# Attention numerators stored head-within-row, product banks tied to set slots of an instruction string, and the output products of the second weights in banks of four and two pieces

## The chip, the cores and the metric

The kernel runs on one core of a Trainium2 chip. The metric is the device time of one launch in microseconds (us). Five engines run their own instruction queues in order: PE (matmul), DVE (vector), ACT (activation), POOL (GpSimd) and SP, which here only issues DMAs. They meet only through semaphores.

## The reference

```python
def mha(x, wqkv, wo):                  # B=1, S=2048, D=512, H=32, Dh=16, float32
    q, k, v = split_heads(x @ wqkv)
    p = softmax(einsum("bhqd,bhkd->bhqk", q, k) * Dh ** -0.5)
    return merge_heads(einsum("bhqk,bhkd->bhqd", p, v)) @ wo

g = sigmoid((x * gate_w).sum(-1, keepdims=True))
out = g * mha(x, wqkv_a, wo_a) + (1 - g) * mha(x, wqkv_b, wo_b)
```

## The kernel before

**The work.** There are 64 heads (32 of each block), in 8 groups G of 8. For a head, two things are done for each tile of 128 tokens, called a round (1024 rounds in all). First the maximum of each query's scores is found: six plain maxima and one paired maximum for two rounds (`max_plain`, L229; `max_rise` and `max_pair`, L236 and L241). ACT and DVE share this. Later the scores are computed again with keys on partitions, shifted by the maxima, and put through Exp on ACT (`score`, L292 and L294). The result is multiplied with V and a column of ones on PE (`attend`, L875), in one PSUM bank `acc`. Rows 0 to 15 of each of four strips of `acc` are numerators, row 16 is the softmax denominator. Each half of a head's queries ends with a copy `ev<-acc` (L898) and a store to a DRAM tensor `od` (L899).

**The maxima's way back.** `max_split` (L252 on DVE, L253 to L255 on POOL) splits half a head's maxima into two fp16 parts. `max_rows` transposes them on DVE (L259), writes them to DRAM (`md<-mt`, L262) and reads them back as two further rows of `q_st` (L265). The scores of that half head wait for them.

**The string.** One pass of the string `FULL` covers four rounds and fixes the order of all engines' work: `e` is one score bank with its Exp (16 in a pass), `m`, `D` and `A` are steps of the maxima, a digit is so many quarters of an `attend`, and `W` (four in a pass) is a slot for one piece of the hidden products. `E` evicts a finished product bank. `W` and `R` also run one entry of `row_ops`, which holds `max_split` and `max_rows`. Every second `e` issues one DMA of the list `waiting`, which I call a drip. The last 14 rounds use the string `LATE`.

**The hidden products.** The generator `hidden` puts the projections of later groups, and then the output products, into the slots `W`. A bank is 8 pieces (L311, L333, L618), collected in the single PSUM buffer `ps_p`; `bank` makes sure that the bank before is evicted before the next begins. Evictions alternate between ACT (L735) and DVE (L736) through `copier`. The output products come in five parts: groups 0 to 3 for each half of the tokens (16 banks of 8 pieces, evicted by `first`), then the second weights' groups 4 and 5 for the upper half (8 banks of 4), 4 to 6 for the lower half (8 banks of 6), and 6 for the upper half (8 banks of 2), all evicted by `more` on DVE (L815). Group 7 is handled in the tail by code of its own (`LAST`).

**What feeds the output products.** `prepared` loads the numerators of a group and half of the tokens (`load_num`: four DMAs into `ot`, four into `o_part`) and the inverse denominators (`load_rb`: four DMAs `rb<-rd`), adds the two key halves on POOL (`add_num`, L608) and multiplies (`normalize`, L612). These DMAs go through the same drip and the same SP queue as `md<-mt` and `q_st<-md`. The access patterns before:

```python
od[g]: [HG, 2, NQ, 32, 512]                                                     # L75
load_num: ap=[[2 * NQ * 32 * 512, 4], [512, DH], [1, 512]]                      # L593
load_rb:  ap=[[S, 4], [0, DH], [1, 512]]                                        # L603
```

Of the kernel before, what the change touches and what calls it, by code (L numbers as in the profile page):

```python
# [23 lines left out]
F32 = mybir.dt.float32  # L24
# [9 lines left out]
P = 128  # L34
# [20 lines left out]
def gated_mha(ctx: ExitStack, tc: tile.TileContext, xT, x, wqkv_a, wo_a, wqkv_b, wo_b, gate_w, out):  # L55
# [76 lines left out]
    def drip_rows(t, src, n, last=KH):  # L132
        waiting.extend((part_rows, t, src, b, k, n) for k in range(0, last, n) for b in HALVES)

    def mark(name):
        flags[name] = now[0]

    flags, now = {}, [0]

# [393 lines left out]
    def load_den(G):  # L533
        o, n = od[G], gh[G] * DH
        for part in range(2):
            dens[G, part] = work.tile([P, P], F32, name=f"dn{part}")
            for c in range(2):
                nc.sync.dma_start(dens[G, part][c * 64:c * 64 + n // 2],
                                  bass.AP(tensor=o.tensor, offset=o.offset + (32 * (2 * part + c) + 16) * 512,
                                          ap=[[NQ * 32 * 512, gh[G] * 2], [P, 4], [1, P]]))  # L540
# [38 lines left out]
    def load_num(G, i):  # L579
        k = SLOTS[G, i]  # L580
        o = od[G]
        for p in range(2):
            for f, b in enumerate((64, 0)):
                for hh in range(2):
                    def one(p=p, f=f, b=b, hh=hh):
                        if (p, f, hh) == (0, 0, 0):
                            nums["p", G, i] = T["late"].tile([P, 2, 512], F32, name="o_part", bufs=2)
                            nums["r", G, i] = T["late"].tile([P, 2, 512], F32, name="rb", bufs=2)
                        nc.sync.dma_start(
                            nums["p", G, i][b:b + 64, hh] if p else T["o"][b:b + 64, k + hh],  # L590
                            bass.AP(tensor=o.tensor,
                                    offset=o.offset + ((4 * hh * 2 + i) * 4 + 2 * p + f) * 32 * 512,
                                    ap=[[2 * NQ * 32 * 512, 4], [512, DH], [1, 512]]))  # L593
                    yield one

    def load_rb(G, i):
        r = rd[G]
        for f, b in enumerate((64, 0)):
            for hh in range(2):
                def one(f=f, b=b, hh=hh):  # L600
                    nc.sync.dma_start(nums["r", G, i][b:b + 64, hh],
                                      bass.AP(tensor=r.tensor, offset=r.offset + 4 * hh * S + i * 1024 + f * 512,
                                              ap=[[S, 4], [0, DH], [1, 512]]))  # L603
                yield one
# [117 lines left out]

    def bank(pieces, evict):
        empty()
        ps = ps_p.tile([P, 512], F32, name="ps_p")
# [17 lines left out]
    def prepared():  # L743
        added = []
        for name, jobs in (("phase", ((0, 0), (1, 0), (2, 0), (3, 0), (0, 1), (1, 1))),
# [3 lines left out]
            for G, i in jobs:  # L749
                yield from until((G + 1) * HG * NT + 26)  # L750
                while len(added) > 1 and now[0] < added[-2] + 3:
                    yield
                waiting.extend((fn,) for fn in (*load_num(G, i), *load_rb(G, i)))
                waiting.append((mark, ("in", G, i)))
                yield from wait(("in", G, i))
                r = now[0] + 6
                at(r, add_num, G, i)
                at(r + 2, normalize, G, i)
                added.append(r)
                flags["ready", G, i] = r + 5  # L760

    def hidden():
# [34 lines left out]
        drip_rows(w_big, wo[0], 1)  # L797
        for G in range(NG, 2 * NG):
# [14 lines left out]
        def more(ps, t):  # L813
            o = T["acc"][:, t]
            dve.scalar_tensor_tensor(o, ps, gate[1][:, t:t + 1], o, op0=ALU.mult, op1=ALU.add)  # L815

# [5 lines left out]
        flags["out", 0, 1] = now[0]  # L822
        drip_rows(w_big, wo[1], 1, 6)
        waiting.append((nc.sync.dma_start, w_big[:DH, 6], wo[1][DM - DH:, :]))
# [55 lines left out]
    def attended(u):  # L880
# [14 lines left out]
        elif h < NH - 1 and w % NT == NT - 1:  # L895
            G, j = divmod(h, HG)
            ev = work.tile([P, 512], F32, name="ev")
            (dve.tensor_copy if w < NT or h == NH - 2 else act.copy)(ev, acc)  # L898
            nc.sync.dma_start(od[G][j, w // NT].rearrange("c r t -> (c r) t"), ev)  # L899

# [15 lines left out]

    FULL = "mDmeE3We1e2me2A1em3em2em2eWE1D2me1m2em2emeW2e1mE1eme4WREReA"
    LATE = "e2We2e2EWe2e2e2EWe2e2E"
# [10 lines left out]
    while r < ROUNDS:  # L929
# [6 lines left out]
        if r % NT == 2 and r // NT + 1 < NH:  # L936
            new_maxima(r // NT + 1)
        scored = bursts = 0
        for code in order:
# [16 lines left out]
            elif code == "W":  # L956
                next(stream, None)
            elif code.isdigit():
                for _ in range(attend_next(int(code))):
# [46 lines left out]
```

## Time and profile before

| | us |
|---|---|
| runs | 2624.59, 2629.59 and 8974.59 |
| median | 2629.59 |
| the profiled execution | 2624.47 |
| its span, first to last instruction | 2622.6 |
| busy in it: PE, DVE, ACT, POOL | 2529.7, 2369.7, 2397.6, 411.5 |

The first launch took 8974.59 us; the median is not touched by it. A busy PE is not PE at its peak, since the ends of matmuls are modelled. ACT and DVE are busy 91% and 90% of the span, so the time is lost in stretches where both wait at once, and the question for each stretch is who waits for whom.

### The profile page before, as it was taken

To read this page: it belongs to the slowest core of one execution; us is meant where nothing else is said; L and a number is where in the kernel's file an instruction comes from. 1 tells how busy PE (TensorE), PEld (TensorE's weight loads), DVE (VectorE), ACT (ScalarE), POOL (GpSimd) and SP (SyncE) were. 2 spreads that over 40 slices of the span, in tenths; PEclk is the share of its full clock that TensorE was granted. 3 is DMA by queue.
4 is the path that set the end of the run, shared out by engine and by line. 5 is a ranking of instruction groups with operands and counts; after the bars stand their busy time and mean duration, and the time that the engine had idled before them with its cause. 6 is when DMAs were issued, how large, how long until landed. Compare 5 with 4: busy or idle time off the path is not lost.

```text
span 2622.6 us, 169689 instructions
## 1 busy us (share of the span) xinstructions
PE 2529.7 (96%) x76566; PEld 1608.1 (61%) x76566; DVE 2369.7 (90%) x4604; ACT 2397.6 (91%) x4741; POOL 411.5 (16%) x809
## 2 busy tenths in 40 slices
PE   8999999999999999999999999989999999899997
PEld 4566766666666666666666666545665665555663
DVE  2889999999999999999999999988899899899994
ACT  1589999999999999999999999989999999899995
POOL 2132211212100000211112111112101100101003
PEclk9899999999999999999999999999999999999999
DMA  7432323222221222323222222223113212212103
GB/s 156 110 85 74 86 65 93 82 71 58 71 60 52 74 65 62 88 73 79 61 66 74 69 62 65 80 89 108 47 50 97 84 50 77 80 54 83 34 27 115
DMA packets 144943, 195.09 MB, mean 74 GB/s; under 512 B 39752, under 2 KB 89880, under 8 KB 144216
## 3 DMA queue, kind: packets, MB, share of 16 engines
q1 hardware_dynamic: 138680, 172.82, 23.1%
q8 instruction: 599, 9.81, 1.6%
q0 software_dynamic: 2560, 8.91, 1.3%
q10 hardware_dynamic: 2976, 2.49, 0.4%
q14 instruction: 128, 1.05, 0.1%
HBM read 117.56 MB, written 66.58 MB: 70 GB/s over the span
## 4 chain that ended last, share of the span: by engine, by line
PE 75%; DVE 11%; DMA 4%; POOL 3%; ACT 3%; issue 2%; SPq 1%; ACTq 0%; POOLq 0%; DVEq 0%
PE acc L875 35%; PE ps_m L223 14%; PE ps_st L292 12%; DVE mxp L229 7%; PE ps_p L311 6%; PE ps_st L223 3%; PE ps_p L618 2%; DMA md<-mt 2%; ACT p L294 2%; PE ps_p L333 1%; DVE ev L898 1%; DVE rise L241 1%; ACT ev L898 1%; POOL stage L771 1%; DMA w<-in_wqkv_a 1%
## 5 line engine op out<-in xcount | busy, mean ns | idle before, releaser
L294 ACT ACTIVATE p<-ps_st 128x512 f32<-128x512 f32 x4068 | 2122.5, 640 | 105.3 <-PE ps_st L292 67.9
L875 PE MATMUL acc<-p,vg 64*17 64x384 f32 (+1 forms) x34784 | 2194.0, 366 | 12.2 <-DVE ev L891 2.4
L229 DVE TENSOR_REDUCE mxp<-ps_m 128x1 f32<-128x512 f32 x3072 | 1942.1, 683 | 89.7 <-PE ps_m L223 61.7
L292 PE MATMUL ps_st<-q_st,k_st 50*32 50x512 f16 x16272 | 1559.2, 382 | 24.1 <-DMA q_st<-md 21.7
L223 PE MATMUL ps_m<-k_st,q_st 48*32 48x512 f16 x14336 | 1384.1, 379 | 24.5 <-DVE mxp L229 20.5
L875 PEld LDWEIGHTS acc<-p,vg 64*17 64x17 f32 x34784 | 975.5, 93 | 236.8 <-DVE ev L898 23.1
L292 PEld LDWEIGHTS <-k_st 50*32 50x32 f16 x16384 | 664.5, 90 | 387.9 <-issue 191.7
L223 PEld LDWEIGHTS <-q_st 48*32 48x32 f16 x16384 | 553.4, 90 | 266.1 <-issue 172.6
L311 PE MATMUL ps_p<-x_sb,w 64*32 64x512 f32 x3648 | 478.2, 591 | 1.3 <-issue 0.8
L241 DVE CUSTOM_DVE_ANT_0 rise<-ps_m,rise 128x512 f32<-128x512 f32 x512 | 349.6, 683 | 64.3 <-PE ps_st L292 56.5
L236 ACT ACTIVATE rise<-ps_st 128x512 f32<-128x512 f32 x512 | 316.3, 618 | 41.7 <-PE ps_st L223 29.5
L618 PE MATMUL ps_p<-w_big,ot 64*32 64x512 f32 x1792 | 234.8, 591 | 14.1 <-DVE o_acc L815 12.2
L223 PE MATMUL ps_st<-x_st,q_st 48*32 48x512 f16 x2048 | 225.5, 379 | 1.1 <-DMA x_st<-xd 1.1
L253 POOL TENSOR_SCALAR mrow<-mrow 128x8 f32<-128x8 f32 x128 | 29.8, 233 | 1233.5 <-DVE mrow L252 1233.1
L357 POOL CAST parts<-stage 128x512 f16<-128x512 f32 x56 | 34.1, 610 | 853.8 <-DVE stage L736 434.2
L311 PE MATMUL ps_p<-w_big,x_sb 64*32 64x512 f32 x1024 | 134.2, 590 | 0.0
L311 PEld LDWEIGHTS ps_p<-x_sb,w 64*32 64x32 f32 x3648 | 116.7, 106 | 17.0 <-DMA w<-in_wqkv_a 1.8
L333 PE MATMUL ps_p<-w_big,x_sb 64*32 64x256 f32 x1280 | 88.6, 382 | 0.1
L618 PEld LDWEIGHTS ps_p<-w_big,ot 64*32 64x32 f32 x1792 | 54.3, 106 | 38.3 <-DVE o_acc L815 17.1
L358 POOL TENSOR_TENSOR parts<-stage,parts 128x512 f16<-128x512 f32 x56 | 65.3, 1165 | 4.5
L333 PEld LDWEIGHTS ps_p<-w_big,x_sb 64*32 64x32 f32 x1280 | 44.1, 107 | 12.8 <-issue 1.0
L898 DVE COPY ev<-acc 128x512 f32<-128x512 f32 x64 | 44.2, 691 | 1.2 <-PE acc L875 0.7
(107 smaller groups left out, 769.2 us busy)
## 6 DMA issues: line engine op xcount, KB each, us to landing
od<-ev SPq DMA_DIRECT2D x126, 256.0 KB
k_st<-kd SPq DMA_DIRECT2D x128, 128.0 KB
q_st<-qd SPq DMA_DIRECT2D x126, 128.0 KB
vd<-v_st SPq DMA_DIRECT2D x64, 136.0 KB
vg<-vd POOLq DMA_DIRECT2D x32, 272.0 KB, 4.1
k_st<-kd SPq DMA_DIRECT2D x128, 64.0 KB
q_st<-qd SPq DMA_DIRECT2D x126, 64.0 KB
kd<-parts SPq DMA_DIRECT2D x56, 128.0 KB
```

What stands on the lines that cost most here:

```text
L223: pe.matmul(ps[j:j + 32], q[b:b + SC, t * P + j:t * P + j + 32], k[b:b + SC], start=True, stop=True, tile_position=(b, j))
L229: dve.tensor_reduce(o[:, c:c + 1], ps, op=ALU.max, axis=AX.X)
L236: act.activation(rises[m], ps, AF.Relu)
L241: dve.tensor_tensor_reduce(out=rise, in0=ps, in1=rise, scale=1.0, scalar=LOWEST, op0=ALU.add, op1=ALU.max, accum_out=o[:, 0:1])
L292: pe.matmul(ps[j:j + 32], k[b:b + SC + 2, kk * P + j:kk * P + j + 32], qv(b), start=True, stop=True, tile_position=(b, j))
L294: act.activation(pt[u][:, c * 512:(c + 1) * 512], ps, AF.Exp, scale=SCALE / UNIT ** 2)
L311: pe.matmul(ps[j:j + 32], a, m, start=k == 0, stop=k == last, tile_position=(b, j))
L333: pe.matmul(ps[j:j + 32, e * 256:(e + 1) * 256], x_sb[b:b + 64, i, k, o:o + 32], w_big[b:b + 64, k, g * P:(g + 2) * P], start=k == e == 0, ...
L358: pool.tensor_tensor(t[:n, 1], v[:n], t[:n, 0], op=ALU.subtract)
L618: pe.matmul(ps[j:j + 32], T["o"][b:b + 64, k, o + j % 64:o + j % 64 + 32], w_big[b:b + 64, g], start=first, stop=last, tile_position=(b, j))
L875: pe.matmul(acc[d:d + 17, qa * P:qb * P], v[b:b + 64, 2 * (w % n) + c if h == NH - 1 else w % n, j], pt[u][b:b + 64, c * 512 + qa * P:c * ...
L898: (dve.tensor_copy if w < NT or h == NH - 2 else act.copy)(ev, acc)
```

## The change

Five edits.

1. `od` of groups 0 to 6 is stored as [half of the queries, half of the heads, strip, row, head, 512]. A partition of `ot` then holds row d and head j as 4d + j instead of 16j + d, and `wo` is loaded in the same order (`wo_rows`). `load_num` needs four DMAs of 256 KB for eight of 128 KB. The first dimension of the DRAM side becomes 64 for the numerators (4 before) and 16 for `rb` (4 before); for the denominators `dn` it becomes 4 (16 before).
2. `max_rows` runs one entry of `row_ops` later: an empty entry stands between `max_split` and `max_rows`.
3. Until the `LATE` string, a bank starts only at the first slot `W` of a pass, or at the third if it has two pieces.
4. The second weights' products become banks of 4 (groups 4 and 5, both halves) and of 2 (group 6, both halves): 32 banks for 24, with the same 96 pieces. `more` alternates between DVE as before and ACT with an addition on POOL.
5. `add_num` and `normalize` are issued together at set rounds, and one `E` of `FULL` moves by a few letters.

```diff
-    od = [dram.tile([HG, 2, NQ, 32, 512], F32, name=f"od{g}") for g in range(2 * NG)]
+    od = [dram.tile([2, 2, NQ, 32, HG // 2, 512], F32, name=f"od{g}") for g in range(2 * NG - 1)]
...
+    def wo_rows(src, b, k):
+        s = src[k * 64:(k + 1) * 64]
+        nc.sync.dma_start(w_big[b:b + 64, k], bass.AP(tensor=s.tensor, offset=s.offset,
+                                                      ap=[[DM, DH], [DH * DM, HG // 2], [1, DM]]))
...
+                    nc.sync.dma_start(dens[G, part][c * 64:(c + 1) * 64], bass.AP(
+                        tensor=o.tensor, offset=o.offset + ((2 * part + c) * 32 + DH) * (HG // 2) * 512,
+                        ap=[[step, 4], [P, DH], [1, P]]))
...
-                            nums["p", G, i][b:b + 64, hh] if p else T["o"][b:b + 64, k + hh],
-                            bass.AP(tensor=o.tensor,
-                                    offset=o.offset + ((4 * hh * 2 + i) * 4 + 2 * p + f) * 32 * 512,
-                                    ap=[[2 * NQ * 32 * 512, 4], [512, DH], [1, 512]]))
+                        nums["p", G, i][b:b + 64] if p else T["o"][b:b + 64, k:k + 2],
+                        bass.AP(tensor=o.tensor,
+                                offset=o.offset + 2 * i * step + (2 * p + f) * 32 * (HG // 2) * 512,
+                                ap=[[512, 64], [step, 2], [1, 512]]))
...
-                                              ap=[[S, 4], [0, DH], [1, 512]]))
+                                              ap=[[0, DH], [1024, HG // 2], [1, 512]]))
...
     def bank(pieces, evict):
+        while not ring and slot[0] % 4 != (2 if len(pieces) == 2 else 0):
+            yield
...
-                while len(added) > 1 and now[0] < added[-2] + 3:
+                while len(added) > 1 and now[0] < added[-2] + 4:
...
-                r = now[0] + 6
+                r = now[0] + 4
+                while r % 8 not in (4, 6) or added and r <= added[-1]:
+                    r += 1
                 at(r, add_num, G, i)
-                at(r + 2, normalize, G, i)
+                at(r, normalize, G, i)
...
         def more(ps, t):
...
+            turn[0] ^= 1
+            if turn[0]:
+                v = T["late"].tile([P, 512], F32, name="added", bufs=2)
+                act.activation(v, ps, AF.Copy, scale=g)
+                pool.tensor_tensor(o, o, v, op=ALU.add)
+            else:
+                dve.scalar_tensor_tensor(o, ps, g, o, op0=ALU.mult, op1=ALU.add)
...
-        yield from wait(("ready", 4, 1), ("ready", 5, 1))
-        yield from outs((4, 5), 1, more)
-        yield from wait(*(("ready", G, 0) for G in (4, 5, 6)))
-        yield from outs((4, 5, 6), 0, more)
-        yield from wait(("ready", 6, 1))
-        yield from outs((6,), 1, more)
+        for i in (1, 0):
+            yield from wait(("ready", 4, i), ("ready", 5, i))
+            yield from outs((4, 5), i, more)
+        for i in (0, 1):
+            yield from wait(("ready", 6, i))
+            yield from outs((6,), i, more)
...
-    FULL = "mDmeE3We1e2me2A1em3em2em2eWE1D2me1m2em2emeW2e1mE1eme4WREReA"
+    FULL = "mDmeE3We1e2me2A1em3em2em2eW1D2mEe1m2em2emeW2e1mE1eme4WREReA"
...
-            row_ops[0:0] = [(max_split, h, f // 8), (max_rows, h, f // 8)]
+            row_ops[0:0] = [(max_split, h, f // 8), (None,), (max_rows, h, f // 8)]
```

In the order of the built programs the change shows at three places on which the prediction rests. (In the changed kernel's rows lines are numbered anew: L252 is L261, L259 is L268, L229 is L238, L898 is L927, L735 is L756.)

The first place is DVE in the steady part, at the second half of head 26 (rows from `max_split`'s reduction `mrow` to the transpose `mt`); before:

```order
L252 TENSOR_REDUCE mrow<-mxp 128x8
L229 TENSOR_REDUCE mxp<-ps_m 128x1
L241 ISA rise,mxp<-ps_m,rise 128x512
L241 ISA mxp 128x1
L229 TENSOR_REDUCE mxp<-ps_m 128x1 x3
L259 STREAM_TRANSPOSE mt<-mparts_225 128x32
```

and with the change:

```order
L261 TENSOR_REDUCE mrow<-mxp 128x8
L238 TENSOR_REDUCE mxp<-ps_m 128x1
L250 ISA rise,mxp<-ps_m,rise 128x512
L250 ISA mxp 128x1
L238 TENSOR_REDUCE mxp<-ps_m 128x1 x7
L268 STREAM_TRANSPOSE mt<-mparts_225 128x32
```

The transpose moves back behind four more maxima.

The second place is SP, at the second half of head 42, where the kernel loads numerators (`ot`, `o_part`), inverse denominators (`rb`) and the next stacks (`k_st`, `q_st<-qd`) around the way back of the maxima; before:

```order
L601 DMA rb<-rd_117 64x1x512 x2
L589 DMA ot<-od_107 64x1x512 x4
L589 DMA o_part<-od_107 64x1x512 x4
L899 DMA od_110<-ev 128x512
L601 DMA rb<-rd_118 64x1x512 x4
L262 DMA md_113<-mt 4x32x32
L265 DMA q_st_211<-md_113 2x1024 x2
L106 DMA k_st_220<-kd_92 32x1x2048
L106 DMA q_st_219<-qd_84 32x1x2048
```

and with the change:

```order
L619 DMA rb<-rd_118 64x1x512 x2
L607 DMA ot<-od_108 64x2x512 x2
L607 DMA o_part<-od_108 64x2x512 x2
L932 DMA od_110<-ev 128x512
L619 DMA rb<-rd_119 64x1x512 x4
L107 DMA k_st_220<-kd_92 32x1x2048
L107 DMA q_st_219<-qd_84 32x1x2048
L271 DMA md_113<-mt 4x32x32
L274 DMA q_st_211<-md_113 2x1024 x2
```

The numerators take half as many DMAs of twice the size, and two loads of the next stacks now stand ahead of `md<-mt`.

The third place is ACT, at the third eviction that it does in the first weights' output products (`o_acc`), with the head's copy `ev`; before:

```order
L898 COPY ev<-acc 128x512
L294 ACTIVATE p<-ps_st 128x512
L236 ACTIVATE rise<-ps_st 128x512
L294 ACTIVATE p<-ps_st 128x512 x8
L236 ACTIVATE rise<-ps_st 128x512
L294 ACTIVATE p<-ps_st 128x512 x5
L735 ACTIVATE o_acc<-ps_p,gate_1578 128x512
L294 ACTIVATE p<-ps_st 128x512 x3
```

and with the change:

```order
L303 ACTIVATE p<-ps_st 128x512 x8
L245 ACTIVATE rise<-ps_st 128x512
L303 ACTIVATE p<-ps_st 128x512 x7
L927 COPY ev<-acc 128x512
L756 ACTIVATE o_acc<-ps_p,gate_1578 128x512
L303 ACTIVATE p<-ps_st 128x512
```

The eviction moves from the middle of a pass to its end, right behind the copy `ev`, which is on ACT in the same passes. On DVE its evictions fall behind DVE's copies `ev` in the same way.

More of the change, by code (lines that the diff above doesn't have):

```diff
@@ L133, in drip_rows, with drip_wo @@
         waiting.extend((part_rows, t, src, b, k, n) for k in range(0, last, n) for b in HALVES)
+    def wo_rows(src, b, k):
+        s = src[k * 64:(k + 1) * 64]
+        nc.sync.dma_start(w_big[b:b + 64, k], bass.AP(tensor=s.tensor, offset=s.offset,
+                                                      ap=[[DM, DH], [DH * DM, HG // 2], [1, DM]]))
+    def drip_wo(src, last=KH):
+        waiting.extend((wo_rows, src, b, k) for k in range(last) for b in HALVES)
     def mark(name):
         flags[name] = now[0]
-    flags, now = {}, [0]
+    flags, now, slot = {}, [0], [0]
     for k in range(0, KH, 2):
@@ L581, in load_num, with one @@
         o = od[G]
+        step = NQ * 32 * (HG // 2) * 512
         for p in range(2):
             for f, b in enumerate((64, 0)):
[L584 to L589, printed above, removed]
-                            nums["p", G, i][b:b + 64, hh] if p else T["o"][b:b + 64, k + hh],
-                            bass.AP(tensor=o.tensor,
-                                    offset=o.offset + ((4 * hh * 2 + i) * 4 + 2 * p + f) * 32 * 512,
-                                    ap=[[2 * NQ * 32 * 512, 4], [512, DH], [1, 512]]))
-                    yield one
+                def one(p=p, f=f, b=b):
+                    if (p, f) == (0, 0):
+                        nums["p", G, i] = T["late"].tile([P, 2, 512], F32, name="o_part", bufs=2)
+                        nums["r", G, i] = T["late"].tile([P, 2, 512], F32, name="rb", bufs=2)
+                    nc.sync.dma_start(
+                        nums["p", G, i][b:b + 64] if p else T["o"][b:b + 64, k:k + 2],
+                        bass.AP(tensor=o.tensor,
+                                offset=o.offset + 2 * i * step + (2 * p + f) * 32 * (HG // 2) * 512,
+                                ap=[[512, 64], [step, 2], [1, 512]]))
+                yield one
     def load_rb(G, i):
@@ L813, in more @@
         def more(ps, t):
-            o = T["acc"][:, t]
-            dve.scalar_tensor_tensor(o, ps, gate[1][:, t:t + 1], o, op0=ALU.mult, op1=ALU.add)
+            o, g = T["acc"][:, t], gate[1][:, t:t + 1]
+            turn[0] ^= 1
[5 more added lines that the diff above has]
+                dve.scalar_tensor_tensor(o, ps, g, o, op0=ALU.mult, op1=ALU.add)
         yield from wait(*(("ready", G, 0) for G in range(4)))
@@ L898, in attended @@
             (dve.tensor_copy if w < NT or h == NH - 2 else act.copy)(ev, acc)
-            nc.sync.dma_start(od[G][j, w // NT].rearrange("c r t -> (c r) t"), ev)
+            o = od[G]
+            if G == LAST:
+                nc.sync.dma_start(o[j, w // NT].rearrange("c r t -> (c r) t"), ev)
+            else:
+                nc.sync.dma_start(o[w // NT, j // 4, :, :, j % 4].rearrange("c r t -> (c r) t"), ev)
     done = [0]
@@ L937, in gated_mha @@
             new_maxima(r // NT + 1)
-        scored = bursts = 0
+        scored = bursts = slot[0] = 0
         for code in order:
@@ L957, in gated_mha @@
                 next(stream, None)
+                slot[0] += 1
             elif code.isdigit():
```

16 lines of the change are left out of this document (12 added, 4 removed).

## The prediction

> **What bounds the kernel now.** I first read the head of the page: how long, and how full the engines are.
>
> ```profile
> span 2622.6 us, 169689 instructions
> PE 2529.7 (96%) x76566; PEld 1608.1 (61%) x76566; DVE 2369.7 (90%) x4604; ACT 2397.6 (91%) x4741; POOL 411.5 (16%) x809
> ```
>
> Three engines are nearly full, so only stretches in which they stop can yield time. A pass of the string has 16 Exps on ACT, so I counted the Exps (L294) in stretches that hold whole passes. The columns are the stretch, its length, ACT's busy time with the count, the clock, and DMA. One Exp crosses a border, so x81 is five passes.
>
> ```profile
> core 0: us, ACT busy (x), PEclk, DMA share, GB/s
> 720.30:1034.10 313.80, 274.32 (x529) 1.00 0.22 59
> 1649.60:1694.50 44.90, 41.74 (x81) 1.00 0.29 94
> 1694.50:1788.20 93.70, 75.25 (x145) 0.95 0.29 91
> 1788.20:1960.10 171.90, 142.05 (x273) 1.00 0.21 64
> 1960.10:2023.10 63.00, 58.82 (x113) 1.00 0.30 97
> 2023.10:2191.80 168.70, 141.96 (x273) 1.00 0.21 66
> 2191.80:2218.90 27.10, 25.05 (x49) 1.00 0.34 102
> 2218.90:2327.80 108.90, 83.29 (x161) 1.00 0.21 65
> 2327.80:2372.40 44.60, 41.86 (x81) 1.00 0.26 88
> 2372.40:2550.60 178.20, 151.15 (x289) 0.99 0.15 45
> ```
>
> Read as us per pass: with all four product slots filled and a bank of 8 evicted in every second pass, 313.8 / 33 = **9.51**. Without products, 44.9 / 5 = 8.98 and 63.0 / 7 = **9.00**. These two are what the string can do. Against them stand the load stretch at 1694 (93.7 / 9 = 10.41 without any product), the first weights' output products (171.9 / 17 = 10.11 and 168.7 / 17 = 9.92), and the second weights' banks of 4 (108.9 / 10 = 10.89) and of 6 and 2 (178.2 / 18 = 9.90). The list of waits (us in all, times, longest) names what is waited for, first over the whole span, then from 1700 to 1800, then in the tail from 2520 on:
>
> ```profile
> PE ps_st L292 <- DMA q_st<-md: 21.7, 7, 6.5
> PEld ps_p L618 <- DVE o_acc L815: 17.1, 13, 2.2
> ...
> PE ps_st L292 <- DMA q_st<-md: 11.6, 3, 6.5
> ...
> PEld L292 <- DMA q_st<-md: 5.4, 1, 5.4
> ```
>
> PE waits for the way back of the maxima (21.7 us: 11.6 in the load stretch, 5.4 in the tail, so 4.7 in the output products), and for evictions of output banks. Each stops ACT and DVE too, since PE's queue is in order.
>
> **Term 1: the transpose one slot later.** The rows are the transpose's waits in all, then one of them at 1112 with POOL before it, then six maxima in a row.
>
> ```profile
> DVE mt L259 <- POOL mparts L255: 20.9, 16, 3.1
> 1112.62 0.18 DVE L252 TENSOR_REDUCE mrow<-mxp 128x8 f32<-128x32 f32 x1
> 1116.90 0.21 DVE L259 STREAM_TRANSPOSE mt<-mparts 128x32 f16<-128x32 f16 x1 [1.11 <-POOL mparts L255]
> 1110.96 0.61 POOL L357 CAST parts<-stage 128x512 f16<-128x512 f32 x1 [16.33 <-DVE stage L736]
> 1116.67 0.20 POOL L255 TENSOR_TENSOR mparts<-mrow,mparts 128x8 f16<-128x8 f32 x1
> 1730.95 3.64 DVE L229 TENSOR_REDUCE mxp<-ps_m 128x1 f32<-128x512 f32 x6
> ```
>
> POOL splits a projection's result from 1110.96 on, so `max_split` ends at 1116.87 and the transpose stalls DVE. It now stands four maxima later, 4 x 3.64 / 6 = 2.4 us. The wait of 1.11 us goes whole. Twelve like it and two of 3.1 us lie in the string, 12 x 1.11 + 2 x 3.1 = 19.5; the other two, ahead of the string and in the tail, make up the 20.9 and stay. The long ones keep 3.1 - 2.4 = 0.7 us each. PE, ACT and DVE run level here, so the rest counts in full, 18.1. I take off 1 us for the four heads where three weight DMAs and now two stack DMAs stand ahead of `md<-mt`: **17.1 us**, between 12 (a third of it hidden elsewhere) and 19.5.
>
> **Term 2: the loads on more DMA engines.** The rows: a transpose, SP's issues behind it, PE's wait, then two stretches (PE, PEld, DVE, ACT, POOL, clock, DMA share, GB/s), then an undisturbed way back.
>
> ```profile
> 1730.82 0.20 DVE L259 STREAM_TRANSPOSE mt<-mparts 128x32 f16<-128x32 f16 x1
> 1730.05 4.48 SPq L601 DMA_DIRECT2D rb<-rd  x4
> 1735.26 0.54 SPq L262 DMA_DIRECT2D md<-mt  x1
> 1744.13 0.53 SPq L265 DMA_DIRECT2D q_st<-md  x2
> 1745.93 0.61 PE L292 MATMUL ps_st<-q_st,k_st 50*32 50x512 f16 x4 [6.46 <-DMA q_st<-md]
> 1730.00:1743.00 13.00, 9.47 (x288) 5.01 (x279) 10.14 (x20) 10.25 (x21) 3.15 (x2) 0.95 0.28 102
> 1746.00:1748.00 2.00, 2.00 (x44) 1.02 (x52) 0.81 (x2) 1.07 (x2) 0.00 (x0) 0.50 0.73 199
> 1757.31 0.20 DVE L259 STREAM_TRANSPOSE mt<-mparts 128x32 f16<-128x32 f16 x1
> 1757.54 0.54 SPq L262 DMA_DIRECT2D md<-mt  x1
> 1759.49 0.53 SPq L265 DMA_DIRECT2D q_st<-md  x2
> ```
>
> `rb`, `ot` and `o_part` flow at 102 GB/s with a DMA share of 0.28, about 4 of 16 engines, as their first dimension of 4 suggests. The stack loads at 1746, whose first dimension is 16, reach 0.73 and 199 GB/s. `md<-mt`, also with a first dimension of 4, stands in line behind the former: 8.87 us from its issue to the next, against 1.95 us undisturbed. After the stop PE runs at a clock of 0.50 for some microseconds. In the change `ot` and `o_part` have a first dimension of 64 and `rb` of 16. One job is 1.5 MB: 15 us at 102 GB/s, 7.5 us at 199, so SP gets rid of it before the next transpose. The stretch at 1694 then costs 9 x 9.00 = 81.0 for 93.7. I keep 1 us of waits: **11.7 us**, between 6 and 13.
>
> What this may cost: the later transpose eats slack. PE needed the rows at 1745.93 - 6.46 = 1739.47, that is 8.65 us after the transpose. The undisturbed way takes 2.18 (1757.31 to 1759.49) + 1.80 (1744.13 to 1745.93) = 3.98. Less 2.4 for the move, 2.3 us are left. The two stack DMAs, now ahead of `md<-mt` in every second half, wait for nothing recent, so SP sends them while the transpose is pending.
>
> The denominators `dn` go the other way, from a first dimension of 16 to 4.
>
> ```profile
> 1662.36 3.09 SPq L538 DMA_DIRECT2D dn<-od  x4
> 1670.38 0.99 POOL L546 TENSOR_TENSOR dn<-dn,dn 64x128 f32<-64x128 f32 x2
> ```
>
> Their user on POOL comes 4.9 us after the issues end. 128 KB at 102 GB/s is 1.3 us, so even three times that is hidden: 0. The Trainium skill (DMA: Bandwidth & Descriptors, section "Why a DMA increments its semaphore by 16 and not by 1") says that a copy runs on the largest number of engines up to 16 that divides the slowest dimension of both sides. By that rule the new loads get 16, and `dn` falls from 16 to 4 engines, the one edit against which it speaks. The trace agrees for the old loads (share 0.28); the sum is the same by rule and row.
>
> **Term 3: the first weights' output products.** Before, a bank ends in the third slot of a pass and the next begins in the fourth, with the eviction between them; PE waits for it. With the change a bank fills two whole passes, as the projections do at 9.51, and is evicted at the end, about a quarter of a pass ahead of the next bank. But every eviction now stands right behind a copy `ev` on the same engine:
>
> ```profile
> L898 ACT COPY ev<-acc 128x512 f32<-128x512 f32 x62 | 38.3, 617 | 0.0
> L735 ACT ACTIVATE o_acc<-ps_p,gate 128x512 f32<-128x512 f32 x8 | 5.5, 682 | 0.0
> L815 DVE SCALAR_TENSOR_TENSOR o_acc<-ps_p,gate,o_acc 128x512 f32<-128x512 f32 x24 | 17.6, 735 | 0.3
> L668 POOL TENSOR_TENSOR o_acc<-o_acc,added 128x512 f32<-128x512 f32 x4 | 5.0, 1268 | 14.8 <-ACT added L667 14.7
> ```
>
> 0.617 + 0.682 = 1.3 us in one burst on ACT every fourth pass, and about as much on DVE. No row shows what this costs. From below it is nothing (9.51); from above, the pass stays at the 9.9 of now. Score banks are three deep, which covers most of a burst, so I take 9.6. Each half then costs 16 x 9.6 + 9.0 for its one empty pass = 162.6: 171.9 + 168.7 - 2 x 162.6 = **15.4 us** (5.8 at 9.9, 18.6 at 9.5). This holds half of the 4.7 us of waits for `md`.
>
> **Term 4: the second weights.** From 2191.8 to 2550.6 stand 36 passes and 358.8 us. With the change these 36 hold 16 passes with a bank of 4, 16 with a bank of 2, and 4 empty ones. A pass with 4 pieces is as full as in term 3: 9.6. With an eviction in each, ACT gets half of the 32 (16 x 0.682 = 11 us); DVE has 16 for 24, so 8 x 0.735 = 5.9 us less; POOL gets 16 x 1.27 = 20 us more, at 16% busy. A pass with 2 pieces lies between 9.0 and 9.6; with its eviction I take 9.3. The sum is 4 x 9.0 + 16 x 9.6 + 16 x 9.3 = 338.4, a gain of **20.4 us** (10.8 at 9.9 and 9.6; 26.8 at 9.5 and 9.0). The tail is not touched: the products end in the changed program two passes earlier, still in `FULL`.
>
> Storing `od` in rows 8 KB apart costs nothing that I can see: the 2 KB pieces stay, and nobody waits for them before the next group.
>
> **Sum.** 17.1 + 11.7 + 15.4 + 20.4 = 64.6. The profiled execution took 2624.47 us; the runs' median is 5 us above it. 2624.5 - 64.6 = 2559.9: I forecast **2560**. With all terms at their ends, 34.6 and 77.9, it is 2547 to 2590.
>
> **The rivals.**
> *The bursts cost what the old waits did.* Terms 3 and 4 fall to 5.8 + 10.8: gain 45.4, 2579. For it: a full pass leaves ACT 9.51 - 9.00 = 0.5 us to catch up, against 1.3. Against it: three score banks each. Chance 0.20.
> *The loads are not spread*, so the edit does not do what it says. Term 2 and the 4.7 us stay, and six waits grow by the 2.4 us of the move: 64.6 - 11.7 - 4.7 - 14.4 = 33.8, 2591. Only the stack rows speak for the spreading of such patterns, and `rb` keeps a repeated row. Chance 0.10.
> *The later transpose makes PE wait in every head* (slower). Where the stack DMAs ahead of `md<-mt` cost its way more than the 2.3 us of slack, every further microsecond is paid in 62 second halves. The change is slower than before from 64.6 / 62 = 1.04 us beyond; at 2 us beyond, 124 us are lost and it ends at 2560 + 124 = 2684 with the clock's drops left out. Against it: 192 KB at 199 GB/s is 1 us, sent ahead of the transpose. Chance 0.05.
> *More than forecast*, 2540 and below, if the terms' upper ends are too low: 0.05. The forecast keeps 0.60.
>
> **Range and chances.** 2538 to 2596 takes in the ends of the sum and the first two rivals. A difference under 2% (here 2577) can hardly be told from no change. Faster: 0.57 of the forecast's 0.60, a third of the first rival, and the last case, 0.68. Slower 0.05; the rest, 0.27, within 2%.
>
> **What would show it.** The transpose's waits fall from 20.9 to about 3 us (term 1). Waits for `q_st<-md` fall from 7 to one or two, the tail's among them, and the share of DMA during loads rises to 0.7 (term 2). Waits of L618 on `o_acc` nearly vanish, and the stretches run at 9.6 and 9.3 us a pass (terms 3, 4). Wrong would be new, regular waits of PE for `q_st<-md` outside the output products, or ACT and PE waiting behind the pairs of copies.

## The result, and the profile after the change

The changed kernel takes 2583.65 us (median of 4 runs, 2576.87 to 2586.85), against 2627.91 us for the kernel before in the same comparison: a ratio of 0.983, with a 95% interval from 0.9806 to 0.9854. That is faster by 1.7%, inside the range of the prediction, but 24 us above its 2560. It is also short of the 2% from which the prediction would have called it faster: this is the outcome to which it gave 0.27. The profiled execution took 2586.85 us, the slowest of the four, and its engines are slightly fuller than before:

```profile
span 2584.8 us, 169617 instructions
...
PE 2532.9 (98%) x76566; PEld 1608.5 (62%) x76566; DVE 2368.4 (92%) x4596; ACT 2404.5 (93%) x4757; POOL 430.2 (17%) x825
```

A pass of the string is named by its first round r here (a pass of `FULL` is four rounds). The next two fences cut each trace at the same passes. The columns are the stretch, its length, the busy time (and count) of PE, PEld, DVE, ACT and POOL, the granted clock, the DMA share, and GB/s. First two stretches of before that the prediction did not show, the projections (r = 2 to 638) and the tail:

```profile
98.50:1649.60 1551.10, 1526.83 (x47883) 1015.52 (x47875) 1460.13 (x2821) 1497.28 (x2962) 260.89 (x545) 1.00 0.26 71
2550.60:2622.60 72.00, 57.34 (x1032) 27.84 (x1019) 35.53 (x73) 41.07 (x80) 21.38 (x27) 0.95 0.30 105
```

Then the changed kernel: the projections, five passes, the nine passes of the first loads, the first weights' passes (r = 698 to 858), the second weights' (r = 862 to 1002), the tail:

```profile
97.10:1630.50 1533.40, 1524.35 (x47878) 1019.13 (x47875) 1461.41 (x2821) 1496.12 (x2961) 260.19 (x545) 1.00 0.27 72
1630.50:1675.10 44.60, 44.23 (x1324) 24.37 (x1320) 44.36 (x92) 44.60 (x92) 9.20 (x17) 1.00 0.49 130
1675.10:1755.80 80.70, 80.64 (x2384) 44.24 (x2367) 78.61 (x155) 80.54 (x165) 21.42 (x22) 1.00 0.39 106
1755.80:2154.80 399.00, 394.20 (x11856) 243.33 (x11855) 372.50 (x722) 382.98 (x758) 44.74 (x94) 1.00 0.25 69
2154.80:2507.80 353.00, 348.09 (x10280) 206.94 (x10287) 331.69 (x642) 339.57 (x675) 53.37 (x92) 1.00 0.22 60
2507.80:2584.80 77.00, 59.12 (x1032) 28.57 (x1031) 35.94 (x73) 41.54 (x80) 21.34 (x27) 0.89 0.28 98
```

Beside the forecast's terms this reads as follows. Before, the first weights' stretch is 171.9 + 63.0 + 168.7 = 403.6 us, the second weights' 358.8.

| stretch | before | forecast | after |
|---|---|---|---|
| projections, 160 passes (term 1) | 1551.1 | 1534.0 | 1533.4 |
| first loads, 9 passes (term 2) | 93.7 | 82.0 | 80.7 |
| first weights, 41 passes (term 3) | 403.6 | 388.2 | 399.0 |
| second weights, 36 passes (term 4) | 358.8 | 338.4 | 353.0 |
| tail | 72.0 | 72.0 | 77.0 |

The head of the program and the five passes ahead of the loads gave 1.4 and 0.3 us more, which makes up the 37.8 us between the spans of the two profiles (44 between the medians, since the profiled execution is the slowest of its four). So the transpose and the loads gave what was forecast, the output products less than a third of it (10.4 us for 35.8), and the tail lost 5 us. The list of waits (us in all, times, longest) shows that the named waits are gone all the same:

```profile
PEld L301 <- DMA q_st<-md: 8.6, 6, 6.5
PE ps_st L301 <- DMA q_st<-md: 6.0, 1, 6.0
PEld ps_p L637 <- ACT o_acc L756: 3.7, 8, 0.5
...
PEld ps_p L637 <- DVE o_acc L757: 3.2, 6, 0.5
...
DVE mt L268 <- POOL mparts L264: 2.2, 4, 0.9
PEld ps_p L637 <- DVE o_acc L844: 2.0, 6, 0.7
```

The transpose waits 2.2 us for 20.9. PE's matmuls wait once for `q_st<-md` instead of seven times, and that one is in the tail; outside it the weight loads wait 2.1 us for it (8.6 less the tail's 6.5). The waits for output banks are 8.9 us in these rows, where the eviction on DVE alone stood at 17.1. What the output products still cost is not in a wait of PE for a bank.

### The profile page after: what moved, and what is told of

It is laid out like the page before. It is cut to its first block, busy times and chain, and to the rows that moved or that the text cites. A ratio compares the mean times of both kernels' runs of the same rounds, so it can differ in the third digit from the quotient of the medians.

```text
span 2584.8 us, 169617 instructions
## 1 busy us (share of the span) xinstructions
PE 2532.9 (98%) x76566; PEld 1608.5 (62%) x76566; DVE 2368.4 (92%) x4596; ACT 2404.5 (93%) x4757; POOL 430.2 (17%) x825
## 4 chain that ended last, share of the span: by engine, by line
PE 85%; DVE 5%; ACT 4%; DMA 2%; issue 2%; SPq 1%; POOL 1%; ACTq 0%; DVEq 0%; POOLq 0%
PE acc L904 39%; PE ps_m L232 16%; PE ps_st L301 15%; PE ps_p L320 6%; PE ps_st L232 3%; DVE mxp L238 3%; PE ps_p L637 3%; ACT p L303 2%; PE ps_p L342 1%; DVE ev L927 1%; ACT ev L927 1%; PE ps_st L320 1%; PE ps_m L320 1%; DMA md<-mt 0%; SPq L107 0%
## 5 line engine op out<-in xcount | busy, mean ns | idle before, releaser
L238 DVE TENSOR_REDUCE mxp<-ps_m 128x1 f32<-128x512 f32 x3072 | 1940.9, 682 | 74.8 <-PE ps_m L232 51.1
L637 PEld LDWEIGHTS ps_p<-w_big,ot 64*32 64x32 f32 x1792 | 57.1, 107 | 21.7 <-ACT o_acc L756 3.7
L842 POOL TENSOR_TENSOR o_acc<-o_acc,added 128x512 f32<-128x512 f32 x16 | 20.4, 1277 | 259.5 <-ACT added L841 259.5
L342 PEld LDWEIGHTS ps_p<-w_big,x_sb 64*32 64x32 f32 x1280 | 43.3, 106 | 11.8 <-issue 1.4
```

Of the source, the lines that this page charges most:

```text
L238: dve.tensor_reduce(o[:, c:c + 1], ps, op=ALU.max, axis=AX.X)
L342: pe.matmul(ps[j:j + 32, e * 256:(e + 1) * 256], x_sb[b:b + 64, i, k, o:o + 32], w_big[b:b + 64, k, g * P:(g + 2) * P], start=k == e == 0, ...
L637: pe.matmul(ps[j:j + 32], T["o"][b:b + 64, k, o + j % 64:o + j % 64 + 32], w_big[b:b + 64, g], start=first, stop=last, tile_position=(b, j))
```

## The experiments

The times below are medians. Since the kernel before itself moved from 2624 to 2630 us between the comparisons, kernels of different comparisons are set side by side by their ratio to it. Stretches are read from one profile each.

**The transpose's place alone, from both sides.** The first kernel is the changed one without the empty place; the second is the kernel before with nothing but that place.

```diff
# e4: undone in the changed kernel
-            row_ops[0:0] = [(max_split, h, f // 8), (None,), (max_rows, h, f // 8)]
+            row_ops[0:0] = [(max_split, h, f // 8), (max_rows, h, f // 8)]
# e12: the only edit of the kernel before
-            row_ops[0:0] = [(max_split, h, f // 8), (max_rows, h, f // 8)]
+            row_ops[0:0] = [(max_split, h, f // 8), (None,), (max_rows, h, f // 8)]
```

> The changed kernel without the empty place between max_split and max_rows, so that the transpose stands where it stood before the change. Theory (term 1, 17.1 us, measured as 16 to 17 us over the projections' passes): +15 to +18 us, about 2600, with DVE's wait for mparts back at about 20 us. Rival (what went in those passes went to the bank places or to E, and the transpose's wait is hidden): within 4 us of the changed kernel.

> The kernel before the change with the empty place between max_split and max_rows as its only edit. Theory (term 1 is worth 16 to 17 us by itself, but with the narrow loads of before the later transpose brings the row to PE too late: 31 us of waits for q_st<-md where the old loads stood under the later transpose, 21.7 us before): -7 to -12 us on the kernel before, about 2616. Rival (the edits don't touch one another): -16 to -18 us, about 2609.

Without the place: 2599.41 us, ratio 0.988 [0.9857, 0.9903], 16 us above the changed kernel (13 by the ratios). The projections' 160 passes are back at 1553.9 us and the transpose at 20.8 us of waits:

```profile
95.60:1649.50 1553.90, 1529.38 (x47878) 1016.06 (x47875) 1460.53 (x2821) 1497.97 (x2962) 260.80 (x545) 1.00 0.26 71
```

```profile
DVE mt L268 <- POOL mparts L264: 20.8, 16, 3.1
```

The place alone: 2619.11 us, ratio 0.9977 [0.9965, 0.9988], only 6 us (3 to 9) below the kernel before. Here are the projections' and the first weights' stretches of the second kernel and its waits:

```profile
97.70:1630.60 1532.90, 1522.27 (x47883) 1017.04 (x47875) 1461.64 (x2821) 1496.06 (x2962) 260.94 (x545) 1.00 0.26 72
1767.60:2180.40 412.80, 398.68 (x11848) 245.36 (x11841) 372.50 (x722) 383.34 (x758) 49.67 (x96) 0.99 0.22 68
```

```profile
PE ps_st L292 <- DMA q_st<-md: 27.9, 13, 5.3
...
DVE mt L259 <- POOL mparts L255: 2.2, 4, 0.9
```

The projections gain 18.2 us by the place alone and lose 20.5 without it. With the old loads PE then waits 13 times for the way back of the maxima, 27.9 us for 21.7, the first weights' stretch takes 412.8 us for 403.6, and two thirds of the gain is gone. The first theory of each holds, though the gain alone is a little under its 7 to 12: the edit is worth 13 to 16 us only where the loads are wide.

**The loads alone.** The changed kernel with the numerators, their loads and the weights' rows as before:

```diff
-    od = [dram.tile([2, 2, NQ, 32, HG // 2, 512], F32, name=f"od{g}") for g in range(2 * NG - 1)]
...
+    od = [dram.tile([HG, 2, NQ, 32, 512], F32, name=f"od{g}") for g in range(2 * NG)]
# load_den, load_num, load_rb, drip_rows for drip_wo, and the store of ev: as before the change
```

> The changed kernel with its first edit alone undone: the numerators lie in DRAM as before, so ot, o_part, rb and the second stage's weights are read with a first dimension of 4 again, in 12 issues a job for 8. Theory (the wide loads gain about 13 us in the nine passes from the first load on, and cost about 10 us, since PE then stops for its own instructions for some 2 us at four places, each in a pass in which the loads move 200 to 360 GB/s): the stretch of the first loads goes back to 10.4 us a pass (+13 us), the waits of PE for q_st<-md come back (some 15 us), and PE's stops in which nothing but issue is named, over 1 us, are gone (-10 us); net +3 to +10 us on the changed kernel, about 2587 to 2594. Rival (the stops come from the later transpose or from another transfer, not from the loads): they stay, and the whole gain of the loads goes: +13 to +20 us, 2597 to 2604.

It took 2610.47 us, ratio 0.9923 [0.9905, 0.9941]: 27 us above the changed kernel (24 by the ratios), more than either theory gave. Its nine passes of the first loads, its first weights' stretch, and its waits:

```profile
1679.40:1770.00 90.60, 82.12 (x2384) 44.51 (x2368) 79.36 (x155) 81.44 (x165) 16.84 (x20) 0.96 0.29 94
1770.00:2182.20 412.20, 396.87 (x11852) 246.00 (x11848) 373.79 (x722) 383.87 (x757) 49.76 (x96) 0.98 0.23 70
```

```profile
PEld L300 <- DMA q_st<-md: 39.4, 18, 5.5
PE ps_st L300 <- DMA q_st<-md: 31.0, 11, 5.0
```

The loads' nine passes lose 9.9 us of the 13.0, the clock falls to 0.96 again, and the first weights' stretch loses another 13.2 us (412.2 for 399.0), with loads in it as well. The wide loads are worth 24 to 27 us together with the later transpose. My theory also said that PE's stops for issue (those for which the profile shows no cause) would go. From the first loads on they nearly do: the longest that PE's list names in this kernel, 1.4 us, stands at 574 us, in the projections. But in the changed kernel they come to about 6 us and not 10; the last section counts them. The passes r = 698 and 702 take 20.5 us for 24.1, but the other kernels with wide loads take 19.5 to 21.4 there, so most of that was one execution of the changed kernel.

**The pairs of copies.** In the steady state of the first weights two things happen every eighth round: a copy `ev`, on DVE and on ACT in turn, and the eviction of a bank, also in turn. In the changed kernel both fall to the same engine. One line exchanges the engines of the evictions:

```diff
         empty()
+        turn[0] ^= 1
         second_phase()
```

> The changed kernel with ACT and DVE exchanged for every eviction of an output bank (the alternation starts on the other engine), all else equal, so that DVE evicts where ACT has just copied ev, and ACT where DVE has. Theory (terms 3 and 4 were lost because the eviction of a bank stands behind a copy ev on the same engine, two in one burst): the cycle of the first weights' products falls from 9.74 us a pass to the 9.47 of the projections, 34 passes, and the second weights' passes by about as much: -9 to -18 us, 2566 to 2575. Rival (ACT and DVE are simply too full in these passes, whichever takes which): the passes stay, within 3 us of the changed kernel.

The rows show the pairs in the changed kernel (first fence), and the same places with the exchange (second fence):

```profile
2125.35 0.60 ACT L927 COPY ev<-acc 128x512 f32<-128x512 f32 x1
2125.81 0.72 ACT L756 ACTIVATE o_acc<-ps_p,gate 128x512 f32<-128x512 f32 x1
...
2105.78 0.69 DVE L927 COPY ev<-acc 128x512 f32<-128x512 f32 x1
2106.39 0.74 DVE L757 TENSOR_SCALAR o_acc<-ps_p,gate 128x512 f32<-128x512 f32 x1
```

```profile
2116.68 0.60 ACT L928 COPY ev<-acc 128x512 f32<-128x512 f32 x1
...
2116.65 0.75 DVE L757 TENSOR_SCALAR o_acc<-ps_p,gate 128x512 f32<-128x512 f32 x1
```

One after the other, the two take 1.3 to 1.4 us of one engine. With the exchange they run at the same moment on two. In the changed kernel ACT stands still for PE behind the pair on DVE, which it does not with the exchange:

```profile
2108.35 3.53 ACT L303 ACTIVATE p<-ps_st 128x512 f32<-128x512 f32 x7 [0.73 <-PE ps_st L301]
```

The four passes r = 834 to 846, first of the changed kernel, then with the exchange, then of a kernel described next (e11), whose evictions are all on DVE:

```profile
2087.90:2126.90 39.00, 38.87 (x1188) 24.76 (x1184) 36.65 (x72) 37.66 (x76) 3.69 (x10) 1.00 0.22 63
```

```profile
2079.70:2117.60 37.90, 37.77 (x1192) 25.16 (x1184) 36.54 (x71) 37.35 (x75) 3.71 (x10) 1.00 0.23 64
```

```profile
2082.90:2121.20 38.30, 38.17 (x1192) 24.98 (x1184) 37.10 (x72) 36.97 (x74) 3.71 (x10) 1.00 0.22 64
```

39.0 us for two pairs and 37.9 for none: a pair costs about 0.5 us here, and the engines' busy times hardly differ. The 38.3 for one pair says little, since the other kernels with the exchange and no pair take 37.9 to 38.4. The first weights' whole stretch and the second weights' with the exchange:

```profile
1758.90:2145.40 386.50, 384.61 (x11860) 246.89 (x11857) 372.56 (x722) 380.10 (x757) 44.87 (x94) 1.00 0.25 71
2145.40:2499.00 353.60, 349.60 (x10280) 206.07 (x10272) 331.71 (x642) 340.12 (x675) 53.77 (x92) 1.00 0.21 60
```

The first falls from 399.0 to 386.5 us, 4.6 of it in the passes r = 698 and 702 (24.1 us for 19.5), which one execution had made long, and 8 in the other 39 by the pairs (16 evictions at 0.5). The second doesn't move (353.6 for 353.0), against the theory. The time, 2582.38 us, ratio 0.9814 [0.9793, 0.9836], does not by itself tell the exchange from the changed kernel. The stretches do: for the 39 passes r = 706 to 858, from one Exp to the same Exp later, seven profiles with the exchange and an alternation give 366.3 to 369.6 us, three without it (the changed kernel, e3 and e4) 374.3 to 375.0. By the means, 368.0 and 374.8, that is 6.8 us, or 0.4 for each of the 16 evictions.

**Which engine evicts.** Four kernels put evictions on DVE: the second weights' 32 in the changed kernel (e3) and with the exchange (e7), and with the cut of banks shown next, its 24 (e10) and all evictions of both weights (e11).

```diff
-            turn[0] ^= 1
-            if turn[0]:
...
+            dve.scalar_tensor_tensor(o, ps, gate[1][:, t:t + 1], o, op0=ALU.mult, op1=ALU.add)
# e11 also, in first:
-            copier(gate[0][:, t:t + 1])(T["acc"][:, t], ps)
+            dve.tensor_scalar(T["acc"][:, t], ps, gate[0][:, t:t + 1], None, op0=ALU.mult)
```

> The changed kernel with all 32 evictions of the second weights on DVE, as before the change; the first weights' keep their alternation. Theory (ACT is the fullest engine, and an eviction on it costs about 1.0 us over a pass without one, on DVE 0.5): 16 passes get 0.5 us cheaper, -8 us, about 2576, with DVE's busy time up 12 us and ACT's down 11. Rival (DVE gets two copies and a reduction more than it can hold, as before the change, and PE waits for its evictions): +5 to +10 us, about 2590, with waits of PE for ps_p on DVE.

> The changed kernel with ACT and DVE exchanged in the first weights' evictions, and all 32 of the second weights on DVE. Theory (the exchange saves 8 us in the first weights' passes by their rows; for the second weights it is the number of evictions that counts and not the engine): first weights at 9.42 us a pass, second weights within 3 us of the changed kernel's 353 us; 2575 to 2580. Rival (ACT is the fullest engine, an eviction costs more there): the second weights' 36 passes fall by 8 us or more, 2568.

> The kernel of banks of 4, then 6 and 2, with all 24 evictions of the second weights on DVE. Theory (an eviction on ACT makes its pass 0.4 to 0.6 us longer than one on DVE: 9.92 against 9.29 and 10.29 against 9.53 in the same passes of earlier runs): 12 evictions x 0.3 to 0.5 = 4 to 6 us less, about 2560. Rival (DVE then gets full, what ACT gains is lost there): within 2 us of 2565.

> As the run before, with the 16 evictions of the first weights on DVE too. Theory (only the pair of an eviction and a copy ev on ACT costs, the pair on DVE nothing: 9.20 us for the pass in which both stand on DVE, 10.04 where both stand on ACT): the first weights' passes go from 9.42 to about 9.33 us, -3 us, about 2557. Rival (two on one engine cost on DVE as well, once ACT takes none): +3 us or more.

They took 2583.26 us (0.9819 [0.9804, 0.9834]), 2572.15 (0.9803 [0.9787, 0.982]), 2568.56 (0.9784 [0.9765, 0.9803]) and 2567.43 (0.9783 [0.9768, 0.9798]). The second weights' 36 passes are 350.3 and 349.4 us in the first two, for 353.0 and 353.6: 3 to 4 us at most, and two kernels that alternate as the changed one does, e4 (without the place) and e8 (with a second one, below), take 350.3 and 350.5 as well. In e10 nothing is left of the 4 to 6 us that I expected against e5, and e11, which brings the pair on DVE back, gives nothing either. That ACT is the fullest engine is not what costs. I dropped this theory.

**Fewer evictions for the same pieces.** Groups 4 and 5 for i = 0 wait for group 6 and share a bank of 6 with it:

```diff
-        for i in (1, 0):
-            yield from wait(("ready", 4, i), ("ready", 5, i))
-            yield from outs((4, 5), i, more)
-        for i in (0, 1):
-            yield from wait(("ready", 6, i))
-            yield from outs((6,), i, more)
+        yield from wait(("ready", 4, 1), ("ready", 5, 1))
+        yield from outs((4, 5), 1, more)
+        yield from wait(*(("ready", G, 0) for G in (4, 5, 6)), ("ready", 6, 1))
+        for t in range(8):
+            yield from outs((4, 5, 6), 0, more, (t,))
+            yield from outs((6,), 1, more, (t,))
```

> The changed kernel with ACT and DVE exchanged in the evictions (as in the run before it that did this alone) and the second weights' banks cut anew: after the 8 banks of 4 of groups 4 and 5 for i = 1, eight pairs of a bank of 6 (groups 4, 5, 6, i = 0) and a bank of 2 (group 6, i = 1), each pair over two passes: 24 evictions for 32 in the same range of passes, 8 passes without products more, and 16 passes with four pieces where there were two. Theory (an eviction costs about its own 0.7 us wherever it stands, since PE, ACT and DVE run in lockstep, and the pieces themselves nearly nothing): 8 x 0.7 = 6 us less, the last 18 passes at 9.7 us as they are, and the 8 emptied passes at 9.0 to 9.1; about 2576. Rival (PE's pieces set the pass): what the emptied passes gain the fuller ones lose, within 2 us of the run with the exchange alone, about 2582.

It took 2564.99 us, ratio 0.9769 [0.9754, 0.9784], the lowest of the kernels that compute the whole result, and 2.3% faster than the kernel before. Its 36 passes, its eight emptied passes (r = 902 to 930), and twelve passes with four pieces and an eviction in each (r = 946 to 990):

```profile
2145.00:2487.90 342.90, 341.14 (x10252) 205.36 (x10247) 327.84 (x637) 335.68 (x670) 45.57 (x83) 1.00 0.22 62
2243.10:2315.10 72.00, 71.70 (x2112) 39.36 (x2112) 70.34 (x141) 71.64 (x148) 9.28 (x19) 1.00 0.33 91
2342.00:2459.30 117.30, 116.67 (x3564) 73.60 (x3564) 111.80 (x214) 114.36 (x226) 10.46 (x26) 1.00 0.14 41
```

The kernel with the exchange alone at the latter twelve passes (two pieces and an eviction in each) and at the former eight (four pieces and an eviction):

```profile
2354.00:2471.50 117.50, 116.35 (x3364) 66.19 (x3360) 110.17 (x214) 113.62 (x226) 11.57 (x27) 1.00 0.14 41
2244.40:2324.70 80.30, 79.61 (x2372) 48.80 (x2360) 75.08 (x147) 76.42 (x152) 13.34 (x23) 1.00 0.30 82
```

The emptied passes cost 72.0 / 8 = 9.00 us, for 80.3 / 8 = 10.0 (the last line). The passes with twice the pieces cost 117.3 / 12 = 9.78, for 117.5 / 12 = 9.79. So pieces beyond the second are free here, and a pass that gets products and an eviction at all is 0.8 to 1.0 us dearer than an empty one. Over the stretch that makes 10.7 us less (353.6 to 342.9), 3 of them in the passes r = 922 and 926, of which the last section tells. The theory holds against its rival, but the pass saved more than the 0.7 us of an eviction; what the rest is, the next two runs show.

**The eviction thin, and left out.** With the exchange, the second weights' evictions work on 32 of 512 columns (the edit shown), or are left out, so that this part of the output is missing:

```diff
+            o, g = T["acc"][:, t, :32], gate[1][:, t:t + 1]
...
+                dve.scalar_tensor_tensor(o, ps[:, :32], g, o, op0=ALU.mult, op1=ALU.add)
```

> The changed kernel with ACT and DVE exchanged in the evictions, and of each of the second weights' 32 evictions 480 of 512 columns left out (ACT, POOL and DVE work on 32 columns), so that this part of the output is missing; products, banks and all else stay. Theory (the 0.7 to 0.8 us that these passes cost over the 9.0 of an empty one are the evictions' own time): the 32 passes come down to 9.1 to 9.3 us each, -14 to -20 us, about 2565. Rival (they are PE's time for the pieces, or the handing over of the bank, which a short eviction pays too): -5 us at most.

> The changed kernel with ACT and DVE exchanged in the first weights' evictions, and all 32 evictions of the second weights left out (their part of the output is missing); the products and banks stay. The run with thin evictions of 32 columns gave 9.44 us for a pass of 2 pieces (a mean over r = 946 to 990), against 9.66 with whole ones and 8.93 with no product at all. Theory (the 0.51 us that are left are the evicting instructions themselves, which hold ACT or DVE and PE's bank even when thin): the passes come down to 8.9 to 9.05 us, the 36 passes by 12 us against the thin run, about 2549. Rival (they are PE's time for the pieces): the passes stay at 9.4, the time at 2560.

They took 2561.43 us (0.9761 [0.9747, 0.9776]) and 2565.15 us (0.9773 [0.9758, 0.9788]). The 36 passes and the twelve passes r = 946 to 990, thin and then without:

```profile
2142.00:2484.60 342.60, 339.89 (x10276) 209.99 (x10261) 323.82 (x642) 332.31 (x674) 37.41 (x92) 1.00 0.22 62
2344.30:2457.60 113.30, 113.06 (x3364) 67.43 (x3360) 107.22 (x214) 110.38 (x227) 5.45 (x27) 1.00 0.14 42
```

```profile
2149.10:2490.90 341.80, 339.41 (x10280) 211.29 (x10271) 320.99 (x626) 330.54 (x659) 33.43 (x76) 1.00 0.22 62
2351.10:2464.00 112.90, 112.64 (x3364) 67.56 (x3360) 106.19 (x208) 109.57 (x221) 3.93 (x21) 1.00 0.14 42
```

A pass with two pieces: 9.79 us with its eviction, 9.44 with a thin one, 9.41 with none, and 9.00 without products. So the 0.8 us split into 0.38 for the eviction, nearly all of it for its columns, and 0.41 for the products. The 9.79 is one profile: the other kernels with all 32 evictions and wide loads take 9.65 to 9.77 there, which leaves 0.24 to 0.36 for an eviction. The first theory was too large (the stretch lost 11 us for 14 to 20), and the second fell: its rival is what happened. What makes two pieces cost as much as four stays open.

**A second empty place.** A test of how much slack the way back of the maxima has left, and of the prediction's slower rival:

```diff
-            row_ops[0:0] = [(max_split, h, f // 8), (None,), (max_rows, h, f // 8)]
+            row_ops[0:0] = [(max_split, h, f // 8), (None,), (None,), (max_rows, h, f // 8)]
```

> The changed kernel with ACT and DVE exchanged in the evictions and a second empty place between max_split and max_rows, so that the transpose stands another four maxima (2.4 us) later. Theory (from the transpose to the row that PE needs there are 6.4 us, and the way back takes 4.0: another 2.4 us use up all of it): waits of PE for q_st<-md in many of the 62 half heads, up to 1 us each, +10 to +50 us. Rival (PE's need moves with it, since the rows ahead of the transpose are late by as much): no waits, within 4 us.

2581.99 us, ratio 0.9838 [0.9824, 0.9853], for 0.9814 with one place. The transpose's wait is 1.2 us, and the waits for `q_st<-md` grow (PE's were 4.4 us, once, with one place):

```profile
PEld L301 <- DMA q_st<-md: 16.2, 13, 5.7
...
PE ps_st L301 <- DMA q_st<-md: 10.1, 8, 5.2
```

Eight waits for the many that I had expected. By the rows of heads 13 to 24 the second place brings the transpose only 1.4 us nearer to PE's need and not 2.4, from 6.4 us ahead of it to 5.0. The way back takes 4.0 us where nothing delays it, so the row still lands 1 us early. My theory, 10 to 50 us more, fell. Of its rival, that PE's need moves with the transpose, 1.0 of the 2.4 us held.

## Why the prediction was right or wrong

**Term 1** held: 17.1 us forecast, 17.7 measured, and the place undone costs 16. The slack was right in the move (9.0 us before, 6.4 after, 2.6 for the 2.4 forecast). The slower rival did not happen.

**Term 2** held: 11.7 us forecast for the nine passes, 13.0 measured. The rival of loads that are not spread is out: they keep the 16 DMA engines 96.7% busy while they flow (last section). The one wait of PE's matmuls for `q_st<-md` that is left is the tail's (6.0 us), as expected. The denominators, read with a first dimension of 4 now, cost nothing, as forecast. Their user on POOL starts 5.3 us after the last issue ends, and does not wait for them there:

```profile
1643.38 2.27 SPq L549 DMA_DIRECT2D dn<-od  x4
```

```profile
1650.94 0.98 POOL L564 TENSOR_TENSOR dn<-dn,dn 64x128 f32<-64x128 f32 x2
```

**Term 3** was mis-sized, 15.4 us forecast and 4.6 measured. The step that failed is the choice between the bounds, 9.6 us a pass because score banks three deep cover most of a burst. The steady cycle was 39.0 / 4 = 9.75. The mechanism had been named (the pairs of copies), as had its sign, ACT and PE waiting behind them, and the exchange shows its price, 0.4 to 0.5 us an eviction: without the pairs the stretch takes 386.5 to 389.7 us in seven profiles, about the forecast's 388.2. Three banks do not cover the burst. PE, ACT and DVE are each busy almost all of such a pass (38.87, 37.66 and 36.65 of 39.0 us), which leaves little room to catch up; that this is why is argued. Of the 10.8 us that are missing the pairs are 7 to 8, and the long passes r = 698 and 702 of this one execution the rest. No run undoes the third and the fifth edit by themselves.

**Term 4** was mis-sized too, 20.4 us forecast and 5.8 measured. The step that failed is that a pass of 2 pieces with its eviction takes 9.3 us, and one of 4 pieces 9.6. 9.4 is the price without an eviction. The 32 evictions add 353.6 - 341.8 = 11.8 us (8 to 12 over the kernels, whose 36 passes take 349.4 to 353.6), and I had booked them as work moved from DVE to ACT and POOL. Eight evictions more than before were counted as a relief. The other 3 us are the passes r = 922 and 926, 22.7 us for two at 9.6.

**The tail** was forecast untouched and took 77.0 us for 72.0; in the twelve kernels of the experiments it took 71.8 to 75.5. From its 38th to its 46th microsecond, the changed kernel, then the exchange with DVE (73.6 us):

```profile
2545.80:2553.80 8.00, 5.63 (x78) 2.91 (x82) 4.82 (x6) 2.94 (x6) 1.27 (x1) 0.62 0.24 77
```

```profile
2532.90:2540.90 8.00, 5.52 (x134) 2.77 (x138) 5.99 (x13) 5.31 (x12) 1.36 (x3) 1.00 0.19 69
```

PE got a clock of 0.62 for 1.00 in these 8 us, with 78 matmuls for 134. Such a stretch is there in some of the kernels and not in others; what sets it off is open.

**The rivals.** The likeliest of them, the bursts at 2579 (chance 0.20), came nearest, 5 us off. It was right for term 3 in kind; for term 4 the cause was the number of evictions and not the pairs, as the exchange shows by moving nothing there.

## What to carry to other kernels

In this kernel, where three engines run level, an eviction of 0.7 us costs 0.24 to 0.38 us of pass time, with little difference between ACT and DVE, and a pass pays 0.4 us for having products at all, two pieces as much as four. So pack the pieces into fewer passes with fewer evictions before distributing them. Two copies of one period belong on two engines at the same moment: flipping one bit did that. And a later transpose and wider loads are one edit: the transpose's place alone gave 6 us, on top of the wide loads 13 to 16.

## What the runs showed of the hardware

PE's own instructions come by DMA too, and can come late. In the changed kernel in pass r = 922 the loads hold the DMA engines, no instructions come, and then PE stops. The DMA queues from 2303.7 to 2309.0, then from 2309.2 to 2311.5, then what the engines did from 2308 on:

```profile
q1 hardware_dynamic: 692, 1.24, 96.7%
```

```profile
q1 hardware_dynamic: 147, 0.03, 6.4%
q8 instruction: 1, 0.02, 3.2%
```

```profile
2308.00:2310.00 2.00, 2.00 (x68) 1.28 (x52) 1.99 (x6) 1.89 (x5) 0.00 (x0) 1.00 0.53 118
2310.00:2312.00 2.00, 0.95 (x26) 0.26 (x18) 0.63 (x2) 0.85 (x2) 0.00 (x0) 1.00 0.04 4
```

```profile
2311.63 0.62 PE L637 MATMUL ps_p<-w_big,ot 64*32 64x512 f32 x2 [1.05 <-issue]
```

For 5.3 us no instruction transfer is among the 692 packets. Then one comes, and PE goes on at 2311.63. By itself the gap says little, since over the whole execution 598 transfers bring 9.80 MB, one in 4.3 us.

What ties the stop to them is its place in the program. 9.80 MB for PE's 2 x 76566 matmuls and weight loads is 64 bytes each, so a transfer holds 256 of them. Counted in order of their start, all 59 waits of PE's matmuls of over 0.5 us between 100 and 2500 us that the 14 traces put down to "issue" stand at one and the same place of such a block of 256, to within one record. In the changed kernel the next transfer starts 0.9 us (median) after PE has passed that place; ahead of the stop at 2311.63 it was 3.3 us, ahead of the longest one (2.2 us, up to 1766) 3.8, and PE stopped at the next block. The Trainium skill (Runtime: NRT & Kernel Launch, section "Instruction fetch mechanics") says that each engine's sequencer fetches its instructions in blocks of 16 KiB through a DMA queue of its own, and that the cost is mostly hidden. The trace agrees on the size (9.80 MB / 598 = 16.4 KB) and shows a place where it is not hidden.

The width of the loads has a part in it: PE's idle times of over 0.2 us at that place, from 1640 to 2500 us, sum to 6.1 us in the changed kernel and to 0.5 in e1, where only the layout and the loads of the numerators are the old ones; the other kernels with wide loads lose 3.5 to 6.3 us there, the other two with the old ones 0.7 and 2.4. It is not the only cause, since every one of these traces has such idle times before the loads as well (1.2 us at 572 in the changed kernel), and the time of the two passes r = 922 and 926 does not show it alone: 22.7 us here, 20.3 with the old loads, and 18.5 where e5 had taken the products out of them.
